# Down products of a gated feed-forward layer: seven products in two pairs of PSUM banks in place of eight, with the order of four engines and the DMA queue given by a table

## The chip, the cores and the metric

The kernel runs on one core of a Trainium2 chip. The core has a matrix engine (TensorE, PE in the profile, with its weight loads as PEld), a vector engine (VectorE, DVE), an activation engine (ScalarE, ACT), a general engine (GpSimd, POOL) and a queue that issues transfers (SyncE, SP). The time is the device time of one execution in microseconds, the median of several runs. All engines run their own instructions in order and wait for each other by semaphores.

## The reference, cut to what matters

The layer mixes an attention branch and a feed-forward branch by a gate `g` per token. There are 2048 tokens of width D = 576, and the hidden width is F = 4608.

```python
g = _sigmoid((x * gate_w).sum(-1, keepdims=True))
a = _A_ref(x, A_wq, A_wk, A_wv, A_wo, A_beta)     # 32 heads, 4 chunks of 512 tokens, a memory carried along
b = (_gelu(x @ w_gate) * (x @ w_up)) @ w_down
return g * a + (1 - g) * b
```

The change is about the last product of `b`, the down product: a 2048 x 4608 matrix (hidden) by a 4608 x 576 matrix (`w_down`), and about how the factor `1 - g` gets onto it.

## The kernel before, in words

Every float32 operand is carried as a pair of 16-bit words, a high one and a low one, and a product is three matmuls: high by high, high by low, low by high. ACT makes the high word (a copy to 16 bits), POOL or DVE the low word (the source minus the high word).

The first part (up to about 210 us) projects queries, keys and values and forms the recurrent memory. The second part is the feed-forward layer with the attention of the 32 heads laid between its work. It is a loop over 72 steps `v`: the hidden width is cut into 36 slices `f` of 128 columns, the tokens into two pairs `p` of chunks of 512, and step `v` has slice `v // 2` and pair `v % 2`. Two slices, so four steps, are a block (`fb` in the code), and there are 18 blocks. The third part multiplies by `wo` and adds the attention branch.

In a step the products of gate and up with both chunks are already formed with seven products in place of eight (names S1 to S4, A11, A12, A22 over the accumulators V, X, Y in the banks V, G, U). Of these, A12 of every block but the first is itself split again into seven products of width 256 in place of eight (`nested`, line 385, with its sums on DVE at lines 1392 to 1406 and its weight sums on POOL at lines 323 to 342). DVE then multiplies gate and up (`hidden`, line 1250), and `hidden_pair` makes the two 16-bit words of each 128 x 512 piece of the hidden matrix (ACT line 1254, POOL line 1255): eight pieces in a block.

The down product of a block runs during the next block. It is 32 chains (`down`): 16 tiles of 128 tokens by two halves of 288 columns, each of six matmuls (two slices by three word products; line 1228) into one bank (`dn`, two buffers). DVE adds each chain into the result `acc` in SBUF, scaled by `ev`, which holds the power-of-two scales and the factor `1 - g` of each token (line 1236).

Beside this lie, in each block: the weights of the next slices (load, sums of squares on ACT line 94, scaling on POOL lines 303, 309 and 432, sums on POOL lines 406 to 410, words on ACT line 418 and POOL line 426; `w_down` words on ACT line 436 and POOL line 440), and four heads, each with two units of scores, softmax and values (scores line 1137, mask and maximum on DVE line 1140, the bound `mb` on ACT line 1150, the exponentials on ACT line 1153, words on ACT line 1163 and POOL line 1164, a transposing transfer on SP, values line 1183, and normalization on DVE lines 1193 to 1200).

The order of the work on PE, ACT, DVE and POOL is the order in which the code of `step` is written (a manual schedule); the DMA queue is ordered by a scheduler.

## Time and profile before

| | |
|---|---|
| Time, median of 3 runs | 1556.04 us (1555.63 to 1557.02) |
| The profiled execution's own span | 1553.8 us |
| PE busy | 1548.4 us (100%) |
| POOL busy | 1305.8 us (84%) |
| DVE busy | 1229.3 us (79%) |
| ACT busy | 1183.7 us (76%) |
| Granted TensorE clock | 1.000 |

The profile was taken from one execution, whose span from the first to the last instruction is 1553.8 us; the median of the runs is 2.2 us above it. A group row gives the line, the engine, the operation, the tiles it writes and reads, the shape and the count; behind the bar the busy time and the mean time of one instruction. An instruction can begin before the one ahead of it on its engine has ended, so the step from start to start can be shorter than the time of one. The steps of the loop repeat block by block: every fourth step begins 72.43 us after the one four before it.

### The profile page before, as it was taken

The page shows a single profiled execution, that of the slowest core. Times are in us where ns is not written, and L with a number is a line of the kernel's source. Part 1 is how long each engine was busy: PE and PEld are TensorE (multiplying, and loading weights), DVE is VectorE, ACT ScalarE, POOL GpSimd, SP SyncE. Part 2 cuts the span into 40 slices and gives each one's busy share as a digit, 9 for nine tenths or more (in the row PEclk, how much of TensorE's full clock was granted, in tenths as well). Part 3 has the DMA queues.
Part 4 walks back from the last instruction along what each step waited for, and adds up shares of the span by engine and source line. Part 5 has one row for each costly group of instructions (what it writes and reads, how often), then busy time and mean ns, then how long its engine had stood idle before and what let it go on. Part 6 is the DMA issues. An engine that isn't in the chain of part 4 may idle for free.

```text
span 1553.8 us, 33925 instructions
## 1 busy us (share of the span) xinstructions
PE 1548.4 (100%) x12195; PEld 955.7 (62%) x12196; DVE 1229.3 (79%) x3198; ACT 1183.7 (76%) x2037; POOL 1305.8 (84%) x1313
## 2 busy tenths in 40 slices
PE   9999999999999999999999999999999999999999
PEld 5665655666666566666666665666666666666577
DVE  6788976778878887878788887878787878887665
ACT  7567544888888888888888888888888888876421
POOL 3544778899898999989899989898999989899597
PEclk9999999999999999999999999999999999999999
DMA  7533341667768687778777878878687878774654
GB/s 254 195 127 125 132 150 34 122 126 140 133 131 141 130 144 130 144 126 137 132 136 126 140 139 136 135 140 151 127 138 133 144 128 141 130 136 99 120 118 138
DMA packets 472601, 210.14 MB, mean 135 GB/s; under 512 B 427632, under 2 KB 437360, under 8 KB 471920
## 3 DMA queue, kind: packets, MB, share of 16 engines
q1 hardware_dynamic: 472432, 207.97, 67.6%
q8 instruction: 96, 1.57, 0.4%
q14 instruction: 73, 0.60, 0.1%
HBM read 92.03 MB, written 27.26 MB: 77 GB/s over the span
## 4 chain that ended last, share of the span: by engine, by line
PE 94%; POOL 3%; ACT 2%; DVE 1%; issue 1%; POOLq 0%
PE dn L1228 27%; PE U L1268 22%; PE V L1268 12%; PE pv L1183 4%; PE G L385 3%; PE st L447 3%; PE dn L454 2%; PE U L1275 2%; PE dn L385 1%; PE U L447 1%; PE V L1280 1%; PE G L1280 1%; PE st L1137 1%; PE G L447 1%; PE st L1669 1%; PE V L1275 1%
## 5 line engine op out<-in xcount | busy, mean ns | idle before, releaser
L1228 PE MATMUL dn<-paird,hh 128*128 128x288 f16 x3396 | 476.5, 286 | 0.2
L1164 POOL TENSOR_TENSOR pf<-pf,ph 128x512 f16<-128x512 f32 (+1 forms) x256 | 359.2, 1403 | 94.6 <-ACT ph L1163 83.6
L1228 PEld LDWEIGHTS <-hh 128*128 128x128 f16 x3456 | 332.2, 98 | 139.1 <-issue 18.1
L1268 PEld LDWEIGHTS <-pairg 128*128 128x128 f16 x2616 | 244.0, 98 | 254.8 <-issue 18.3
L1236 DVE SCALAR_TENSOR_TENSOR acc<-dn,ev,acc 128x288 f32<-128x288 f32 x534 | 274.4, 515 | 51.4 <-PE dn L1228 42.9
L1153 ACT ACTIVATE pf<-pf,mb,esc 128x512 f32<-128x512 f32 (+3 forms) x512 | 293.0, 642 | 5.2
L1268 PE MATMUL U<-xt,pairg 128*128 128x512 f16 x864 | 209.9, 379 | 0.2 <-DVE gl L1459 0.2
L1268 PE MATMUL U<-x,pairg 128*128 128x512 f16 x840 | 204.1, 379 | 0.0
L426 POOL TENSOR_TENSOR pairg<-raw,pairg 128x640 f16<-128x640 f32 (+2 forms) x144 | 176.2, 1239 | 3.0 <-ACT pairg L418 1.5
L1163 ACT ACTIVATE ph<-pf 128x512 f16<-128x512 f32 (+1 forms) x256 | 172.4, 720 | 0.0
L1255 POOL TENSOR_TENSOR hh<-gl,hh 128x512 f16<-128x512 f32 x144 | 164.4, 1163 | 7.5 <-ACT hh L1254 7.5
L1140 DVE CUSTOM_DVE_ANT_0 pf<-st,mask 128x512 f32<-128x512 f32 (+1 forms) x256 | 157.2, 614 | 0.0
L418 ACT ACTIVATE pairg<-raw 128x640 f16<-128x640 f32 (+2 forms) x144 | 89.3, 647 | 56.6 <-POOL raw L410 36.2
L1258 ACT ACTIVATE gl<-gl,sc 128x512 f32<-128x512 f32 x144 | 97.2, 716 | 40.7 <-DVE gl L1505 30.1
L303 POOL TENSOR_SCALAR raw<-raw,sc 128x640 f32<-128x640 f32 x72 | 118.7, 1663 | 0.0
L1459 DVE COPY gl<-U 128x512 f32<-128x512 f32 x72 | 49.8, 692 | 85.4 <-PE U L1268 74.9
L1150 ACT ACTIVATE mb<-mx,esc 128x4 f32<-128x4 f32 x128 | 37.5, 293 | 103.4 <-DVE mx L1140 103.4
L1140 DVE CUSTOM_DVE_ANT_0 pf<-dn,mask 128x256 f32<-128x256 f32 (+1 forms) x192 | 67.2, 375 | 55.3 <-PE dn L1137 55.3
L1268 PE MATMUL V<-xt,pairg 128*128 128x512 f16 x432 | 105.7, 381 | 0.0
L1268 PE MATMUL V<-x,pairg 128*128 128x512 f16 x432 | 104.8, 378 | 0.0
L1254 ACT ACTIVATE hh<-gl 128x512 f16<-128x512 f32 x144 | 82.6, 616 | 16.0 <-DVE gl L1250 15.8
L1183 PEld LDWEIGHTS <-pt 128*128 128x128 f16 x2560 | 83.4, 96 | 12.3
(354 smaller groups left out, 2971.1 us busy)
## 6 DMA issues: line engine op xcount, KB each, us to landing
raw<-in_wgu_dram SPq DMA_DIRECT2D x36, 640.0 KB
rawd<-in_wd_dram SPq DMA_DIRECT2D x36, 288.0 KB
qk<-stage SPq DMA_DIRECT2D x36, 256.0 KB
qt<-qk SPq DMA_DIRECT2D x128, 72.0 KB
kt<-qk SPq DMA_DIRECT2D x128, 72.0 KB
...
qt<-qk SPq DMA_DIRECT2D x128, 36.0 KB
```

The source lines that it names most:

```text
L303: pool.tensor_scalar(r, r, scl[f // 2][0][:, 0:1], None, OP.mult)
L426: pool.tensor_tensor(spot(f, *p, 1), raw_g[f][:, p[0] : p[1]], spot(f, *p, 0), OP.subtract)
L1140: dve.tensor_tensor_reduce(prob[a][:, COL[qi] : COL[qi] + (qi + 1) * P], out[qi], mask[:, L - (qi + 1) * P :], 1.0, -3e38, OP.add, OP.max, ...
L1153: act.activation(r, r, AF.Exp, bias=b[:, qi : qi + 1], scale=esc[:, 0, c : c + 1])
L1163: act.activation(h[:, cols], p[:, cols], AF.Copy)
L1164: pool.tensor_tensor(p.bitcast(F16)[:, cols], p[:, cols], h[:, cols], OP.subtract)
L1183: pe.matmul(ov, pr[:, 10 * i + COL[qi] // P + kb], v[:, 4 * e + kb, c0 : c0 + VC], start=kb == 0 and i == 0, stop=kb == qi and i == 1)
L1228: pe.matmul(o[:, :NH], hh[:, a, q * P : (q + 1) * P], w[:, b, n * NH : (n + 1) * NH], start=i == 0, stop=i == 5)
L1236: dve.scalar_tensor_tensor(av, o[:, :NH], ev, av, OP.mult, OP.add)
L1255: pool.tensor_tensor(hh[:, 1], t, hh[:, 0], OP.subtract)
L1258: act.activation(t, o, AF.Gelu_apprx_tanh, scale=scl[f // 2][0][:, 2 + c : 3 + c])
L1268: pe.matmul(o, w[:, i, (a + k) * P : (a + k + 1) * P], x[:, b + k], start=start and k == 0 and i == 0 and b == h, stop=k == 1 and i == 1, ...
```

## The change: what it does

**Down product.** The pieces of the hidden matrix of a block are, for each chunk pair, a 2 x 2 arrangement (two chunks by two slices), and so are the two slices of `w_down` (two slices by two column halves). The change multiplies them with seven products in place of eight. The sums on the hidden side are four subtractions or additions of 128 x 512 float32 tiles on DVE for each pair (`sums_h`: S3, S2, S1, S4), both inputs in SBUF; the sums on the weight side are four of 128 x 288 on POOL (`down_weights`: t1 to t4). Each of the seven operands on either side gets its two words: on the hidden side 14 in a block on ACT (line 1290) and POOL (line 1294), on the weight side 7 of 128 x 288 in a block (lines 1349 and 1352).

**Banks.** A product (`multiply`) takes two tiles of 128 tokens at once, six matmuls of width 288 into the two banks of a pair: P1, P6, P7 and P4 into the pair `two`, P5, P3 and P2 into the pair `st2`. In each pair the next product is added on top of the one before it in PSUM, and after every product DVE adds what stands there into one quadrant of `acc` (`evict`, 128 x 2 x 288, line 1328). The two pairs of banks replace the banks `dn` and `st`, and the scores of the heads use them too.

**Gate at the end.** The scale in an eviction is now one number per chunk (`we`), and the factor `1 - g` is multiplied into `acc` at the end by 16 activations on ACT (`weigh`, line 1672).

**What moves between engines.** The second split of A12 is dropped: A12 is six matmuls of width 512 again, and a copy from bank G to bank U on DVE stands where the nested sums were. The scaling of the weights goes from POOL to ACT (lines 331 and 372). The bound `mb` goes from ACT to DVE as a three-operand instruction with a constant tile in SBUF (line 1094). The scratch `z` of the scale computation moves from SBUF into a PSUM bank. Loading a head's queries and keys is 12 transfers in place of 8. Some of the output stage's sums go from POOL to DVE.

**Order.** The work of a block is cut into 341 named units, and a table gives their order, with an offset of blocks for units of the block before or after. The order holds for PE, ACT, DVE, POOL and now the DMA queue up to unit A12.1 of the last block, and behind that the scheduler orders all; the output stage's first 14 steps may start between the last down products.

```diff
+ORDER_OF_BLOCK = """
+S3.0 ldg.1 P1.00+1 EP1.00+1 h1.3+1 mb.6+1 sq1.1 tr.5+1 pH.A11.1+1 A11.0 P2.00+1 EP2.00+1 P6.00+1 EP6.00+1
+wL.T3+1 ldd.0 cY.0 va.4+1 P2.01+1 pL.A22.0+1 pH.A22.1+1 wL.T4+1 e3.6+1 pL.S3.1+1 P7.00+1 pH.S1.0+1 cV.0
...
         if fb:
...
-            ev = wts.tile([P, 16], F32, name="ev", tag="ev", bufs=2)
-            pool.tensor_tensor(ev.rearrange("p (c q) -> p c q", c=4),
-                               gate[:, 1].rearrange("p (c q) -> p c q", c=4),
-                               w.unsqueeze(2).to_broadcast([P, 4, 4]), OP.mult)
-            evs[fb - 1] = ev
+            ev = evs[fb - 1] = wts.tile([P, 4], F32, name="we", tag="we", bufs=4)
+            pool.tensor_scalar(ev, scl[fb - 1][1][:, 0], v[:, 0, 1:2], 2.0**35, OP.mult, OP.mult)
...
+    def scale_g(f, parts=(0, 1)):
         if f < NF:
+            for i in parts:
+                r = raw_g[f][:, i * KW : (i + 1) * KW]
+                act.activation(r, r, AF.Copy, scale=scl[f // 2][0][:, 0:1])
...
     def scale_d(f):
         r = raw_d[f]
-        pool.tensor_scalar(r, r, scl[f // 2 + 1][0][:, 1:2], None, OP.mult)
+        act.activation(r, r, AF.Copy, scale=scl[f // 2 + 1][0][:, 1:2])
...
+        def bound(a):
+
+            b = bounds[a] = ap_.tile([P, 4], F32, name="mb", bufs=2)
+            c = 2 * (a // (2 * H)) + a % 2
+            dve.scalar_tensor_tensor(b, mx.pop(a), esc[:, 1, c : c + 1], ln256, OP.mult, OP.add)
...
-        def down(fb, t, n):
-            c, q = divmod(t, 4)
-            o = spare()
-            i = 0
-            for f in (2 * fb, 2 * fb + 1):
-                w = pair_d[f]
-                hh = hp[f, c]
-                for a, b in ((0, 0), (0, 1), (1, 0)):
-                    pe.matmul(o[:, :NH], hh[:, a, q * P : (q + 1) * P], w[:, b, n * NH : (n + 1) * NH],
-                              start=i == 0, stop=i == 5)
-                    i += 1
-            av = acc[:, t, n * NH : (n + 1) * NH]
-            ev = evs[fb][:, t : t + 1]
...
-                dve.scalar_tensor_tensor(av, o[:, :NH], ev, av, OP.mult, OP.add)
...
+            def copy_y():
+                s["Y"] = bank("U")
+                dve.tensor_copy(s["Y"], s["X"])
...
+            def third():
+                a, d = made[b, p, 0, 0], made[b, p, 0, 1]
+                h["A11"], h["S3"] = a, d
+                dve.tensor_tensor(d, a, d, OP.subtract)
+
+            def second():
+                h["S2"] = h["S3"]
+                dve.tensor_tensor(h["S2"], made[b, p, 1, 1], h["S3"], OP.subtract)
+
+            def one():
+                h["S1"] = h["A11"]
+                dve.tensor_tensor(h["S1"], h["S2"], h["A11"], OP.add)
+
+            def fourth():
+                h["S4"] = made[b, p, 1, 0]
+                dve.tensor_tensor(h["S4"], h["S4"], h["S2"], OP.subtract)
...
+        SEVEN = {"P1": ("A11", "B11", 0, 0), "P6": ("S2", "T2", 0, 1), "P7": ("S3", "T3", 1, 1), "P4": ("A22", "T4", 1, 0),
+                 "P5": ("S1", "T1", 1, 1), "P3": ("S4", "B22", 0, 1), "P2": ("A12", "B21", 0, 0)}
...
+            def multiply(m):
+                o = two if m in ("P1", "P6", "P7", "P4") else st2
+                x, w = as_pair(hp[b, p, SEVEN[m][0]]), wp[b, SEVEN[m][1]]
+                for j in range(2):
+                    for k, (g, h) in enumerate(((0, 0), (0, 1), (1, 0))):
+                        pe.matmul(o[:, j, :NH], x[:, g, (q + j) * P : (q + j + 1) * P], w[:, h],
+                                  start=k == 0 and m in ("P1", "P5", "P2"), stop=k == 2, skip_group_check=True)
+
+            def evict(m):
+                e, to = SEVEN[m][2:]
+                t = 4 * (2 * p + e) + q
+                o = two if m in ("P1", "P6", "P7", "P4") else st2
+                o, av = o[:, :, :NH], acc[:, t : t + 2, to * NH : (to + 1) * NH]
+                ev = evs[b][:, 2 * p + e : 2 * p + e + 1]
+                if (t, to) in begun:
+                    dve.scalar_tensor_tensor(av, o, ev, av, OP.mult, OP.add)
...
+            for n, k in enumerate((("B12", "B12", "B11"), ("B22", "B22", "B12"), ("B11", "B22", "B11"), ("B21", "B21", "B22"))):
+                add(f"t{n + 1}", lambda k=k: minus(*k))
...
+        def weigh(ts):
+            for t in ts:
+                act.activation(acc[:, t], acc[:, t], AF.Copy, scale=gate[:, 1, t : t + 1])
...
+        with tc.manual_schedule(engines=ORDERED | {mybir.EngineType.SP}):
+            for k in todo[first:free]:
+                run(k)
```

**Where instructions stand.** VectorE in the middle of a block, before the change. `acc<-dn` is a down eviction, `pf` and `mx` are the masked scores and their maximum, `gl<-U` and `gl<-V` are sums of the gate and up products.

```order
L1236 SCALAR_TENSOR_TENSOR acc<-dn,ev,acc 128x288
L1140 ISA pf_2624,mx<-dn,mask 128x256
L1140 ISA mx 128x1
L1505 TENSOR_TENSOR gl<-U,gl 128x512
L1514 TENSOR_TENSOR gl<-V,gl 128x512
L1140 ISA pf_2624,mx<-pv,mask 128x128
L1140 ISA mx 128x1
L1236 SCALAR_TENSOR_TENSOR acc<-dn,ev,acc 128x288
L1140 ISA pf_2624,mx<-st,mask 128x512
L1140 ISA mx 128x1
L1236 SCALAR_TENSOR_TENSOR acc<-dn,ev,acc 128x288 x2
```

VectorE behind the scores of a unit, after the change. Line 1094 is the bound `mb`, line 1271 the sum S3 of a chunk pair (both inputs are hidden tiles in SBUF), line 1240 the sums of the gate and up products, line 1328 a down eviction.

```order
L1094 SCALAR_TENSOR_TENSOR mb<-mx,esc,ln_76 128x4
L1271 TENSOR_TENSOR hh_2619<-hh_2623,hh_2619 128x512
L1240 TENSOR_TENSOR hh_2621<-U,hh_2621 128x512
L1240 TENSOR_TENSOR hh_2630<-V,hh_2630 128x512
L1328 SCALAR_TENSOR_TENSOR acc<-two_2650,we,acc 128x2x288
L1141 TENSOR_REDUCE pv<-pv 128x144
L1142 RECIPROCAL ord<-pv 128x8
L1145 SCALAR_TENSOR_TENSOR pv<-pv,gha,ord 128x72 x2
L1148 TENSOR_TENSOR ob<-ob,pv 128x8x18
L1328 SCALAR_TENSOR_TENSOR acc<-two_2650,we,acc 128x2x288
L1271 TENSOR_TENSOR hh_2620<-hh_2629,hh_2620 128x512
L1175 SCALAR_TENSOR_TENSOR hh_2630<-G,sc,hh_2630 128x512
```

The evictions are fewer and twice as wide, and between them stand two kinds of instruction that VectorE did not have: the sums of hidden tiles and the bound.

GpSimd at the beginning of a step, before the change. Line 1255 is the low word of a hidden piece, line 303 the scaling of a slice's weights, line 1164 the low words of the attention weights, lines 426 and 336 the low words of the weights and of the second split's sums, lines 406 and 407 the weight sums.

```order
L1255 TENSOR_TENSOR hh_2618<-gl,hh_2618 128x512
L1255 TENSOR_TENSOR hh_2620<-gl,hh_2620 128x512
L303 TENSOR_SCALAR raw<-raw,sc 128x640
L303 TENSOR_SCALAR raw<-raw,sc 128x256
L1164 TENSOR_TENSOR pf_2625<-pf_2625,ph 128x512
L1164 TENSOR_TENSOR pf_2625<-pf_2625,ph 128x768
L426 TENSOR_TENSOR pairg_11843<-raw,pairg_11843 128x640
L426 TENSOR_TENSOR pairg_11843<-raw,pairg_11843 128x384
L336 TENSOR_TENSOR pairg_11843<-nu_2804,pairg_11843 128x128
L406 TENSOR_TENSOR raw<-raw 128x256
```

GpSimd at the turn from one block to the next, after the change. Line 1294 is the low word of a hidden piece or sum, line 1352 that of a down weight, line 1355 a sum of down weights, lines 1112 and 368 the low words of the attention weights and of the gate and up weights.

```order
L1294 TENSOR_TENSOR hh_2626<-hh_2619,hh_2626 128x512
L1355 TENSOR_TENSOR rawd_2331<-rawd_2332,rawd_2331 128x288
L1112 TENSOR_TENSOR pf_2655<-pf_2655,ph 128x768
L1352 TENSOR_TENSOR wp_2643<-rawd_2331,wp_2643 128x288
L1352 TENSOR_TENSOR wp_2637<-rawd_2331,wp_2637 128x288
L1294 TENSOR_TENSOR hh_2632<-hh_2621,hh_2632 128x512
L1352 TENSOR_TENSOR wp_2641<-rawd_2332,wp_2641 128x288
L1294 TENSOR_TENSOR hh_2635<-hh_2620,hh_2635 128x512
L368 TENSOR_TENSOR pairg_9891<-raw,pairg_9891 128x640
```

The scaling instructions are gone from the queue, and the low words and sums of the down product have taken their places.

883 lines of the change are left out of this document (419 added, 464 removed).

## The prediction

> **What bounds the kernel now.** I read the page's busy shares first, then the busy time of two neighbouring blocks, then the chain of work that ended last inside one.
>
> ```profile
> span 1553.8 us, 33925 instructions
> PE 1548.4 (100%) x12195; PEld 955.7 (62%) x12196; DVE 1229.3 (79%) x3198; ACT 1183.7 (76%) x2037; POOL 1305.8 (84%) x1313
> ```
>
> ```profile
> core 0: us, PE busy (x) PEld busy (x) DVE busy (x) ACT busy (x) POOL busy (x), PEclk, DMA share, GB/s
> 410.00:482.43 72.43, 72.43 (x604) 44.24 (x603) 59.20 (x163) 61.90 (x106) 65.90 (x65) 1.00 0.71 135
> 482.43:554.86 72.43, 72.43 (x604) 44.21 (x603) 59.19 (x163) 61.90 (x106) 65.86 (x65) 1.00 0.76 134
> ```
>
> PE is busy all through a block at full clock; POOL has 6.5 us of slack in it, ACT 10.5, DVE 13.2. A busy PE need not be at its peak, so its pace is read from the chain, which is all PE there:
>
> ```profile
> 427.96 1.29 PE U L1268 x6
> 429.47 2.24 PE dn L1228 x18
> 469.41 0.66 PE G L385 x6
> ```
>
> A matmul of width 512 takes 0.215 us from start to start, one of 288 0.124, one of 256 0.11: the rows follow each other without holes. PE sets the time, and only less PE work can shorten the loop, as long as no other engine then needs more than PE.
>
> **PE, what goes and comes.** Of the block's 32 x 6 = 192 matmuls of width 288, 168 stay (4 x 7 products of six): 24 x 0.124 = 2.98 us less. The second split of A12 goes: 42 matmuls of width 256 (4.6 us) become 24 of 512 (5.2 us), 0.5 us more. Block: 72.43 - 2.98 + 0.54 = **70.0 us**. Everything else on PE stays.
>
> **DVE.** Its rows, by shape, and four rows of the timeline for the step from start to start:
>
> ```profile
> L1236 DVE SCALAR_TENSOR_TENSOR acc<-dn,ev,acc 128x288 f32<-128x288 f32 x534 | 274.4, 515 | 51.4 <-PE dn L1228 42.9
> L1250 DVE SCALAR_TENSOR_TENSOR gl<-U,sc,gl 128x512 f32<-128x512 f32 x72 | 53.7, 746 | 3.1 <-PE U L1275 3.1
> L1505 DVE TENSOR_TENSOR gl<-U,gl 128x512 f32<-128x512 f32 x72 | 49.5, 687 | 7.6 <-PE U L1280 5.3 <-PE U L1275 2.4
> L1405 DVE TENSOR_TENSOR nu<-U,nu 128x512 f32<-128x512 f32 x34 | 23.5, 692 | 6.7 <-PE U L1268 6.6
> L1396 DVE TENSOR_TENSOR G<-U,nu 128x256 f32<-128x256 f32 x34 | 14.7, 432 | 1.2
> L1197 DVE SCALAR_TENSOR_TENSOR pv<-pv,gha,ord 128x72 f32<-128x72 f32 x128 | 38.5, 301 | 4.6
> ```
>
> ```profile
> 299.34 0.69 DVE L1505 TENSOR_TENSOR gl<-U,gl 128x512 f32<-128x512 f32 x1
> 299.95 0.68 DVE L1514 TENSOR_TENSOR gl<-V,gl 128x512 f32<-128x512 f32 x1
> 300.75 0.51 DVE L1234 TENSOR_SCALAR acc<-dn,ev 128x288 f32<-128x288 f32 x1
> 301.18 0.68 DVE L1140 CUSTOM_DVE_ANT_0 pf<-st,mask 128x512 f32<-128x512 f32 x1
> ```
>
> An instruction costs 0.08 us less than it lasts when another follows: 0.61 at 512, 0.43 at 288. Removed in a block: 32 evictions, 13.8 us; the sums of the second split, two steps of five at 256 (10 x 0.43) and two steps of two at 512 (4 x 0.70), 7.1 us. Added: 28 evictions of 576 elements. From 288 to 512 an instruction grows by 0.231 us, so 576 lasts 0.81 and costs 0.73: 20.5 us. Four copies from G to U and eight sums of hidden tiles at 0.61: 7.3 us. Eight bounds of four elements, by the row of 72 elements less 0.07: 0.23 each, 1.9 us. Sum: 59.2 - 20.9 + 29.7 = **68.0 us** before any wait of a new kind. That is 2 us under PE, where it was 13.
>
> **The new kind of wait.** The eight sums and eight bounds are DVE instructions with two tensors from SBUF; nearly all others on DVE read at most one from there. The kernel before has few of these, and they show what happens beside POOL:
>
> ```profile
> 413.09 0.73 POOL L406 TENSOR_TENSOR raw<-raw 128x256 f32<-128x256 f32 x1
> 413.55 0.90 DVE L1212 SCALAR_TENSOR_TENSOR oh<-ob,wsc,oh 128x576 f16<-128x576 f32 x1
> 413.91 1.13 POOL L407 TENSOR_TENSOR raw<-raw 128x256 f32<-128x256 f32 x1
> ```
>
> ```profile
> L1212 DVE SCALAR_TENSOR_TENSOR oh<-ob,wsc,oh x16: 809/898/1052, 413.5 to 1447.0; 128x576 f16<-128x576 f32 x16
> L486 DVE SCALAR_TENSOR_TENSOR xt<-acc,xsc,xt x6: 1275/1556/1940, 111.2 to 192.1; 128x1024 f16<-128x1024 f32 x6
> L267 DVE TENSOR_SCALAR pb<-z x19: 170/1080/1116, 160.9 to 1435.0; 128x4 int32<-128x4 int32 x19
> ```
>
> Line 1212 begins while POOL is inside line 406 and lasts 0.90 us in place of 0.81; POOL's next one, begun beside it, lasts 1.13 in place of 0.73. Line 486 lasts 1.28 to 1.94. The two hold each other up: the one that comes second waits for the first to end, and 0.18 of the wait is hidden in the beginning of the DVE instruction (POOL ends 0.27 behind its start, it loses 0.09). Even four elements can lose 0.91 us (line 267, of another kind, with one tensor). The price per instruction lies between 0 and 0.91; nearest are 0.09 (line 1212, the only one inside the loop) and 0.28 (line 486, middle of its six). I take the mean, 0.19, for all sixteen: 3.0 us, so **DVE needs 71.0 us**, more than PE. It becomes the bound. Since PE and DVE then release each other's banks with hardly any slack, I add 0.6 us, the middle between nothing (before, PE never waited) and 1.2 (an estimate: one eviction and a half): **71.6 us a block**.
>
> The Trainium skill's page "SBUF — State Buffer", section "Who interferes with whom", states this as a rule: a VectorE instruction with two SBUF inputs and a GpSimd instruction that reads SBUF exclude each other for a whole instruction, whoever begins first. The rows of lines 486 and 1212 agree. By that rule the bounds of four elements wait just as long as the sums; if instead only wide ones waited, the sum for DVE would be 69.5 us, below PE.
>
> **POOL and ACT, which could take over.**
>
> ```profile
> L1255 POOL TENSOR_TENSOR hh<-gl,hh 128x512 f16<-128x512 f32 x144 | 164.4, 1163 | 7.5 <-ACT hh L1254 7.5
> L303 POOL TENSOR_SCALAR raw<-raw,sc 128x640 f32<-128x640 f32 x55 | 103.4, 1890 | 0.0
> L432 POOL TENSOR_SCALAR rawd<-rawd,sc 128x576 f32<-128x576 f32 x36 | 61.6, 1723 | 0.0
> L426 POOL TENSOR_TENSOR pairg<-raw,pairg 128x384 f16<-128x384 f32 x36 | 33.5, 931 | 0.0
> L440 POOL TENSOR_TENSOR paird<-rawd,paird 128x576 f16<-128x576 f32 x36 | 46.0, 1279 | 0.0
> L323 POOL TENSOR_TENSOR junk<-raw 128x128 f32<-128x128 f32 x17 | 8.5, 502 | 0.0
> ```
>
> ```profile
> L1254 ACT ACTIVATE hh<-gl 128x512 f16<-128x512 f32 x144 | 82.6, 616 | 16.0 <-DVE gl L1250 15.8
> L418 ACT ACTIVATE pairg<-raw 128x640 f16<-128x640 f32 x72 | 52.5, 729 | 38.6 <-POOL raw L410 36.2 <-POOL raw L303 2.4
> L436 ACT ACTIVATE paird<-rawd 128x576 f16<-128x576 f32 x36 | 23.9, 667 | 0.0
> L1150 ACT ACTIVATE mb<-mx,esc 128x4 f32<-128x4 f32 x128 | 37.5, 293 | 103.4 <-DVE mx L1140 103.4
> ```
>
> POOL loses the scaling (by width about 7.8 us, and 2 x 1.72), the second split's six small instructions (some 3.2), two low words of `w_down` (2.6) and the gate's `ev` (0.2): 17.2. It gains six low words more (7.0), seven of width 288 (0.76 each by the rows at 384 and 576: 5.3) and four sums of that width (about 0.8: 3.2): 15.5. So 64.2, and with eight sums of DVE that hold it up by 0.4 each, 67.4 us. ACT gains six high words (3.7), seven of width 288 (0.43: 3.0), four scalings of 640 (2.9) and two of 576 (1.3); it loses the bounds (2.3), two words of `w_down` (1.3) and two of the split (0.8): 61.9 + 6.5 = 68.4 us. Both stay under 71.6 but above 94% of it, so a late DVE also makes them late: POOL's low word waits for DVE's sum, and PE's product for the low word.
>
> **Costed at nothing.** In the block of the scales, `z` in PSUM takes away one wait like line 267's, but the next instruction of four elements stands in SBUF and meets it. Twelve transfers a head in place of eight move the same bytes; DMA is busy 0.71 to 0.76, and what hides them is that a head is loaded a block ahead. Behind a transposing transfer in SP's queue wait the loads of heads and weights; if that cover is gone, PE waits at the values.
>
> **Ends.** The loop with heads is 16 blocks. The last block's steps have no heads, and PE bounds them: 2.4 us less. The last down products stand alone behind the gates: 28 x 0.745 for 32 x 0.745, 3.0 less; the 16 activations for the gate and the chain sum, high word, low word, product at the end cost between nothing and 6 us, since the output stage's first steps stand between: I take 3. Together 2.4 less.
>
> **Sum.** 1553.8 + 16 x (71.6 - 72.43) - 2.4 = 1538.1 us of span; the median lies 2.2 above the profiled span, so 1540.3: forecast **1541 us**, 1.0% faster. For this case alone, 1525 to 1552.
>
> **Rivals.**
> *Slower: DVE waits anywhere inside POOL's instructions.* POOL has 65 instructions in 65.9 us, 1.0 us each, and is busy nine tenths of the time. Starts that fall anywhere in them meet half of one, 0.5 us, less the hidden 0.18: 0.32 each, 5.1 a block. DVE then needs 73.1, and with 0.6 for handing over 73.7: 1553.8 + 16 x 1.3 - 2.4 + 2.2 = 1574 us. It decides from 0.25 us per instruction on, where 68.6 + 16 x 0.25 meets the old block. For it: line 486's upper half. Against it: the loop repeats exactly, so each instruction meets POOL at one phase, and line 1212's costs 0.09. At 0.375 each it is 1588. Chance 0.39. This is what the page's rule gives if nothing lines the two engines up.
> *Full gain: PE stays the bound.* If the waits fall into the 2 us that DVE has, a block is 70.0 and 0.3 for handing over: 16 x 2.1 less, 1520 us. Against it: DVE had 13 us of slack when PE never waited. Chance 0.13.
> *No change*, the waits near 0.25: 1553 to 1559. Chance 0.09.
> *The banks as a loop of their own*: a product (0.75), the way to DVE (0.2), an eviction (0.81) and the way back follow one another on the pair `two`, 16 x 1.85, and eight scores at some 1.2: 39 us of 70. This is not a bound, and I give it no chance of its own.
> That the change doesn't do what it says is excluded by the count: the new order has 3024 down matmuls for 3456.
>
> **How the numbers follow.** Forecast 0.39, full gain 0.13, no change 0.09, slower 0.39. A measurement of this kernel tells about 0.2% from no change. Faster 0.52, same 0.09, slower 0.39. The range goes from below the full gain, 1516, to the slower case at 0.375 us per wait, 1588.
>
> **What would show it.** In the block: PE busy falling below the block's length, with waits of PE for DVE at the down products; DVE busy above 95%; the sums (line 1271 and the three behind) and the bounds (line 1094) lasting longer than 0.69 and 0.23 us, by 0.19 in the mean; POOL near 67 and ACT near 68 us. If sums and bounds show their bare times and PE still waits, the reason is another: the order of the table or a late transfer. If PE is busy throughout, the full gain came.

## The result and the profile after

The changed kernel takes 1605.7 us (median of 4 runs, 1603.1 to 1611.4), the kernel before 1556.5 beside it: ratio 1.032 (95% interval 1.031 to 1.034), so 3.2% slower where 1.0% faster was forecast; also outside the range. The profiled execution has a span of 1600.9 us, 47.1 more than before.

```profile
span 1600.9 us, 32993 instructions
PE 1547.9 (97%) x11458; PEld 868.6 (54%) x11458; DVE 1451.2 (91%) x3249; ACT 1304.4 (81%) x2197; POOL 1291.7 (81%) x1308
```

PE is as long busy as before, with 737 matmuls fewer, and now stands still for 53 us. A yardstick that both kernels have is the copy of accumulator V from PSUM on DVE (line 1339 before, line 1217 after; "V copy" below), once in each step. Read by it the 47.1 us are:

| Stretch | before | after | difference |
|---|---|---|---|
| start, to the copy in the first step of the second block | 251.5 us | 261.9 us | +10.4 |
| 16 blocks | 1159.9 us | 1165.2 us | +5.3 |
| the last three steps | 52.1 us | 56.4 us | +4.3 |
| from the last copy to the end | 90.3 us | 117.4 us | +27.1 |

The yardstick itself has moved. In the first step of every block the new order puts the copy 7.5 to 7.7 us behind the start of the product that it copies (before: 1.6 to 1.8), so some 6 of the 10.4 us are the copy's new place and no lost time; they are missing in the third row. The starts of that product don't have this fault (those of the second block and of the last step; before, then after):

```profile
249.96 1.46 PE L1268 MATMUL V<-xt,pairg 128*128 128x512 f16 x6
1461.52 1.47 PE L1268 MATMUL V<-xt,pairg 128*128 128x512 f16 x6
```

```profile
254.44 1.46 PE L1185 MATMUL V<-xt,pairg 128*128 128x512 f16 x6
1480.55 1.47 PE L1185 MATMUL V<-xt,pairg 128*128 128x512 f16 x6
```

By them the start lost 4.5 us, the 16 blocks 5.3 as in the table, the last three steps 9.2 and the time behind them 28.1.

**A block.** The busy time of two neighbouring blocks, columns as in the prediction:

```profile
406.97:479.73 72.76, 72.01 (x563) 39.05 (x561) 70.52 (x164) 67.94 (x113) 66.28 (x66) 1.00 0.67 134
479.73:552.50 72.77, 71.39 (x559) 38.71 (x557) 70.23 (x163) 67.46 (x112) 65.74 (x66) 1.00 0.60 132
```

Most blocks last 72.75 us, some 73.3. Laid out by starts of matmuls, the first of these blocks has 68.5 us of matmuls at their own pace (before: 70.8), 2.8 us of holes where the height of the operands changes (before: 1.6) and 1.5 us of waits (before: none). So 2.4 us came out of the block, as forecast, and 2.7 came in.

The changes of height are seen in the timeline of PE (start, duration, line, shape). Before:

```profile
425.40 0.38 PE L1275 MATMUL U<-x,pairg 128*128 128x512 f16 x1
425.71 0.39 PE L1280 MATMUL V<-x,pairg 64*128 64x512 f16 x1
425.72 0.39 PE L1280 MATMUL U<-x,pairg 64*128 64x512 f16 x1
425.94 0.38 PE L1137 MATMUL st<-kt,qt 54*128 54x512 f16 x2
```

After:

```profile
522.08 0.38 PE L1192 MATMUL U<-x,pairg 128*128 128x512 f16 x1
522.39 0.39 PE L1197 MATMUL V<-x,pairg 64*128 64x512 f16 x1
522.39 0.39 PE L1197 MATMUL U<-x,pairg 64*128 64x512 f16 x1
522.71 0.91 PE L1318 MATMUL two<-wp,hh 128*128 128x288 f16 x6
```

The height is the number of rows of a matmul's operands. From a matmul of 128 rows to one of 64 the step is 0.31 us in place of 0.215, in both kernels. Before, the scores with their 54 rows always stood directly behind, at 0.22. After, a down product with 128 rows follows 6 times of 8, at 0.32, and most scores stand alone and pay for a change of their own. The table cut these neighbours apart; that is 1.2 us a block, summed from the longer steps (no run puts the neighbours back). (The Trainium skill's page "TensorEngine Tiling (Array Packing)", section "Key Properties", says that changing the tiling mode drains the engine. The rows agree where 128 rows stand beside 64 or 54, at 0.10 us a change; from 64 to 54 rows nothing is lost, 0.22 for 0.215.)

**The end.** PE's waits from 1440 us on (before: none at all):

```profile
PE two L1318 <- DVE acc L1328: 12.7, 9, 6.7
PE G L1615 <- DVE hh L1175: 5.6, 1, 5.6
PE V L1615 <- DVE acc L1624: 3.9, 1, 3.9
PE pv L1615 <- POOL x L1608: 2.0, 1, 2.0
PE V L1185 <- DVE hh L1217: 1.2, 2, 1.0
PE two L1318 <- POOL wp L1352: 1.2, 1, 1.2
```

They sum to 28.7 us with the small ones. The longest, with the slow matmuls behind it, is most of the 9.2 us of the last three steps; nearly all the others fall behind the last V copy. The longest is followed back through three queues, PE, DVE and SP:

```profile
1449.43 1.64 PE L1318 MATMUL two<-wp,hh 128*128 128x288 f16 x12
1458.24 3.04 PE L1318 MATMUL two<-wp,hh 128*128 128x288 f16 x12 [6.66 <-DVE acc L1328]
```

```profile
1446.46 1.54 DVE L1283 TENSOR_TENSOR hh<-hh,hh 128x512 f32<-128x512 f32 x1
1456.69 0.17 DVE L1551 TENSOR_SCALAR wst<-wst 128x5 f32<-128x5 f32 x1 [8.69 <-ACT junk L120]
1457.38 1.53 DVE L1328 SCALAR_TENSOR_TENSOR acc<-two,we,acc 128x576 f32<-128x576 f32 x2
```

```profile
1440.17 12.79 SPq L1546 DMA_DIRECT2D raw<-in_wo_dram x3
```

Line 1551 scales the sums of squares of `wo`. It needs ACT's squares, these need the load of `wo`, and the load's third part waits 11.2 us until POOL's words of the weights have freed its buffer. Behind the 128 x 5 instruction stand the evictions that PE waits for. In the kernel before, the engines keep the order of the code at the end too; here the scheduler put the instruction there.

The wait costs twice. Twelve down matmuls last 1.64 us ahead of it and 3.04 behind it, and the windows show the granted TensorE clock as a share of full speed (the third number from the end):

```profile
1450.00:1455.00 5.00, 1.58 (x29) 1.30 (x28) 0.00 (x0) 2.59 (x6) 5.00 (x6) 1.00 0.26 56
1455.00:1460.00 5.00, 1.76 (x8) 1.14 (x8) 2.94 (x6) 1.23 (x3) 0.94 (x1) 0.52 0.67 137
1510.00:1515.00 5.00, 2.11 (x9) 1.24 (x9) 2.74 (x4) 0.63 (x1) 5.00 (x7) 0.50 0.33 106
1535.00:1540.00 5.00, 5.00 (x22) 3.16 (x21) 3.79 (x6) 1.71 (x3) 4.39 (x5) 0.50 0.31 59
```

The clock is 0.50 to 0.52 behind each of the three longest waits (6.66, 5.62 and 3.88 us), and behind the fourth, 3.48 us at 1493, the 3.4 us from 1492.8 are at 0.50 too. In the kernel before it is 1.00 to the end. The Trainium skill's page "TensorE: Matmul & The Clock Gate", section "What's actually happening", gives the rule: half the clock behind an idle window of about 3.4 us, for about as long. These four waits agree. A run below shows that a shorter wait, 2.75 us, can be enough.

**The new kind of wait.** One line of code each, durations min/median/max in ns:

```profile
L1271 DVE TENSOR_TENSOR hh<-hh,hh x36: 677/934/1664, 243.1 to 1469.7; 128x512 f32<-128x512 f32 x36
L1283 DVE TENSOR_TENSOR hh<-hh,hh x36: 675/1324/1540, 256.3 to 1524.6; 128x512 f32<-128x512 f32 x36
L1094 DVE SCALAR_TENSOR_TENSOR mb<-mx,esc,ln x128: 211/492/1503, 281.1 to 1433.3; 128x4 f32<-128x4 f32 x128
L1328 DVE SCALAR_TENSOR_TENSOR acc<-two,we,acc x488: 798/808/821, 259.9 to 1560.2; 128x576 f32<-128x576 f32 x163
L303 DVE TENSOR_SCALAR pb<-pb x19: 155/157/162, 160.7 to 1466.1; 128x4 int32<-128x4 int32 x19
```

```profile
L1094 DVE SCALAR_TENSOR_TENSOR mb<-mx,esc,ln 128x4 f32<-128x4 f32 x128 | 60.4, 472 | 1.7
L1283 DVE TENSOR_TENSOR hh<-hh,hh 128x512 f32<-128x512 f32 x36 | 46.2, 1283 | 1.1 <-POOL hh L1294 1.1
L1271 DVE TENSOR_TENSOR hh<-hh,hh 128x512 f32<-128x512 f32 x36 | 37.3, 1035 | 0.0
L1279 DVE TENSOR_TENSOR hh<-hh,hh 128x512 f32<-128x512 f32 x36 | 35.5, 987 | 0.0
L1275 DVE TENSOR_TENSOR hh<-hh,hh 128x512 f32<-128x512 f32 x36 | 28.6, 795 | 0.0
```

A sum (lines 1271 to 1283) lasts 1.03 us in the mean, 0.35 over its shortest; a bound (line 1094) 0.47, 0.26 over its shortest. With eight of each that is 4.9 us a block. The eviction lasts 0.81, always.

### The profile page after: what moved, and what is told of

It reads as the page before. It is cut to its first block, busy times and chain, and to the rows that moved or that the text cites. A ratio compares the mean times of both kernels' runs of the same rounds, so it can differ in the third digit from the quotient of the medians.

```text
span 1600.9 us, 32993 instructions
## 1 busy us (share of the span) xinstructions
PE 1547.9 (97%) x11458; PEld 868.6 (54%) x11458; DVE 1451.2 (91%) x3249; ACT 1304.4 (81%) x2197; POOL 1291.7 (81%) x1308
## 4 chain that ended last, share of the span: by engine, by line
ACT 32%; PE 30%; DVE 13%; issue 8%; POOL 7%; DMA 5%; SPq 4%; POOLq 0%; ACTq 0%
ACT pf L1101 9%; PE two L1318 7%; PE U L1185 5%; ACT ph L1108 4%; DVE acc L1328 3%; ACT L1178 3%; ACT hh L1178 3%; SPq L1040 3%; PE G L1185 3%; PE V L1185 2%; DVE pf L1083 2%; ACT hh L1290 2%; DMA kt<-qk 2%; POOL pf L1112 2%; ACT L1101 2%
## 5 line engine op out<-in xcount | busy, mean ns | idle before, releaser
L1318 PE MATMUL two<-wp,hh 128*128 128x288 f16 x3024 | 438.6, 288 | 28.3 <-DVE acc L1328 23.6
L1328 DVE SCALAR_TENSOR_TENSOR acc<-two,we,acc 128x576 f32<-128x576 f32 x488 | 385.5, 810 | 9.7 <-PE two L1318 8.5
L1294 POOL TENSOR_TENSOR hh<-hh,hh 128x512 f16<-128x512 f32 x252 | 313.5, 1253 | 8.7 <-ACT hh L1290 8.6
L1101 ACT ACTIVATE pf<-pf,mb,esc 128x384 f32<-128x384 f32 (+3 forms) x512 | 298.6, 642 | 17.2 <-POOL hh L1294 8.4
L1083 DVE CUSTOM_DVE_ANT_0 pf<-two,mask 128x384 f32<-128x384 f32 (+2 forms) x448 | 210.5, 511 | 3.6 <-PE two L1080 3.6
L1185 PE MATMUL G<-x,pairg 128*128 128x512 f16 x864 | 209.9, 379 | 0.5 <-DVE hh L1175 0.5
L368 POOL TENSOR_TENSOR pairg<-raw,pairg 128x640 f16<-128x640 f32 (+2 forms) x144 | 178.3, 1240 | 14.3 <-ACT pairg L363 14.3
L1290 ACT ACTIVATE hh<-hh 128x512 f16<-128x512 f32 x252 | 151.2, 615 | 17.1 <-DVE hh L1279 9.2
L1178 ACT ACTIVATE hh<-hh,sc 128x512 f32<-128x512 f32 x144 | 99.8, 715 | 37.8 <-DVE hh L1456 19.4
L1101 ACT ACT_TABLE_LOAD x64 | 82.1, 1283 | 52.6 <-issue 52.0
L1352 POOL TENSOR_TENSOR wp<-rawd,wp 128x288 f16<-128x288 f32 x126 | 99.7, 803 | 11.2 <-ACT wp L1349 11.1
L1185 PE MATMUL U<-x,pairg 128*128 128x512 f16 x432 | 105.1, 379 | 1.3 <-DVE hh L1467 0.8
L1178 ACT ACT_TABLE_LOAD x65 | 83.4, 1283 | 1.2
```

The costliest lines, as they stand in the source:

```text
L368: pool.tensor_tensor(spot(f, *p, 1), raw_g[f][:, p[0] : p[1]], spot(f, *p, 0), OP.subtract)
L1083: dve.tensor_tensor_reduce(prob[a][:, COL[qi] : COL[qi] + (qi + 1) * P], out[qi], mask[:, L - (qi + 1) * P :], 1.0, -3e38, OP.add, OP.max, ...
L1101: act.activation(r, r, AF.Exp, bias=bounds[a][:, qi : qi + 1], scale=esc[:, 0, c : c + 1])
L1178: act.activation(t, o, AF.Gelu_apprx_tanh, scale=scl[f // 2][0][:, 2 + c : 3 + c])
L1185: pe.matmul(o, w[:, i, (a + k) * P : (a + k + 1) * P], x[:, b + k], start=start and k == 0 and i == 0 and b == h, stop=k == 1 and i == 1, ...
L1290: act.activation(as_pair(hp[b, p, k])[:, 0], of(k), AF.Copy)
```

## The experiments

All are edits of the changed kernel. "Rest" is the time from the last V copy to the end in the profile; the changed kernel has 117.4 us there and a usual block of 72.75. The loop varies from execution to execution: in the profiles of the runs that change the end alone its 16 blocks take 1164.7 to 1169.4 us, and 1176.5 in one that has a block of 80.3. Differences of a few us in the whole time therefore say little; blocks and rests say more.

### The loop: is VectorE the bound?

**The eight sums left out.**

```diff
 def third():
-    dve.tensor_tensor(d, a, d, OP.subtract)
+    pass
 # and the same in second, one, fourth
```

> The changed kernel without the eight sums of hidden tiles on VectorE (S3, S2, S1 and S4 of both chunk pairs are left out; the words are made of the unsummed tiles). VectorE is rid of eight instructions of 1.03 us in the mean, from start to start about 0.97, so 7.8 us a block, among them the chain from sum to sum. Theory 'VectorE sets the block': the block falls to what TensorE needs, 70.0 to 70.6 us, over 16 blocks 34 to 44 us: 1562 to 1572 us. Rival 'the order and the ways set it': less than half of that, above 1586 us.

Measured: 1606.8 us (ratio 1.031 to 1.034). A block:

```profile
479.70:552.40 72.70, 72.08 (x563) 39.02 (x562) 64.19 (x156) 67.76 (x112) 63.36 (x66) 1.00 0.59 130
```

DVE has 6 us less to do and the block is as long as ever. PE's waits sum to 1.5 us as before, in other places. DVE's total is not the bound. (The rest is 124.3 us here, 6.9 longer; what lengthens it isn't known.)

**The four scalings of the gate and up weights on ACT left out.**

```diff
 def scale_g(f, parts=(0, 1)):
-    act.activation(r, r, AF.Copy, scale=scl[f // 2][0][:, 0:1])
+    pass
```

> The changed kernel without the four scalings of the gate and up weights on ScalarE (line 331 is left out; the words are made of the unscaled weights). ScalarE is rid of four instructions of 0.73 us, 2.9 us a block; three of them lie where ScalarE waits for the next unit's exponentials soon after. Theory 'way from engine to engine': the block falls by less than 0.7 us, since the scalings do not lie on the chain: above 1592 us. Rival 'ScalarE is full' (66.5 us of instructions and 10.3 us of table loads and waits in 72.75): the block falls by what is taken away until TensorE bounds it, to 71.2 us or less, 1578 to 1582 us.

Measured: 1605.7 us (1.030 to 1.033). ACT is busy 64.9 us in a block of 73.30, and blocks last 73.3 to 73.8: no shorter, with less work. Blocks of 73.3 are no sign of the edit: the run below with eight products in the last block alone has the changed kernel's loop and shows them in 10 of its 16 blocks. ACT's total isn't the bound either.

**The bound back on ACT**, undoing that part alone.

```diff
-dve.scalar_tensor_tensor(b, mx.pop(a), esc[:, 1, c : c + 1], ln256, OP.mult, OP.add)
+act.activation(b, mx.pop(a), AF.Copy, bias=LN256, scale=esc[:, 1, c : c + 1])
```

> The changed kernel, with the bound of the exponentials on ScalarE again as in the kernel before, in place of VectorE. VectorE is rid of eight instructions of 0.46 us in the mean (3.7 us a block), ScalarE gains about eight times 0.27 (66.5 to 68.7 us a block). Theory 'VectorE with its waits for GpSimd sets the block': the block falls from 72.75 to between 70.4 and 71.3 us (TensorE needs 70.0), over 16 blocks 23 to 38 us: 1568 to 1583 us. Rival 'the order of the table and the way from engine to engine set it': the block stays within 0.4 us of 72.75, or grows because the exponentials now wait for ScalarE: above 1598 us.

Measured: 1654.3 us (1.058 to 1.068), most blocks 75.4, some 77 and 82. In this order of the work, made for DVE, the move to DVE helps.

**The bound with one tensor from SBUF.**

```diff
-dve.scalar_tensor_tensor(b, mx.pop(a), esc[:, 1, c : c + 1], ln256, OP.mult, OP.add)
+dve.tensor_scalar(b, mx.pop(a), esc[:, 1, c : c + 1], LN256, OP.mult, OP.add)
```

> The changed kernel with the bound of the exponentials on VectorE as an instruction with one tensor from SBUF and a constant as second operand, in place of two tensors (line 1094, four elements). What it tells is what such a small instruction waits for beside GpSimd. If only instructions with two tensors from SBUF and GpSimd exclude each other, line 1094 lasts 0.15 to 0.25 us throughout in place of 0.21 to 1.50 (mean 0.46), and VectorE is rid of 2 us a block; if one tensor waits as well (line 267 of the kernel before did, up to 1.12 us), it lasts as before. The time: by the theory 'way from engine to engine' up to 0.7 us a block less, since the bound lies on the chain at two places, 1594 to 1606 us; if it waits as before, 1602 to 1608 us.

Measured: 1608.9 us (1.029 to 1.038), and the bound waits just as long:

```profile
L1094 DVE TENSOR_SCALAR mb<-mx,esc x128: 218/504/1504, 281.0 to 1441.4; 128x4 f32<-128x4 f32 x128
```

So the second tensor is not what makes it wait.

**The maxima in PSUM**, in four columns of the banks `two` that the scores leave free, and the bound with one tensor.

```diff
-mx[a] = ap_.tile([P, 4], F32, name="mx", bufs=2)
+mx[a] = two[:, a % 2, 500:504]
```

> The changed kernel with the four maxima of a unit kept in PSUM (columns 500 to 503 of the pair two, which nothing else uses) in place of SBUF, and the bound made of them by one operand and a constant, so that it reads no tensor from SBUF. The waits of the bound for GpSimd should vanish: line 1094 lasts 0.47 us in the mean (0.21 to 1.50) and should last 0.15 to 0.25. Theory 'the bound's waits lie on the way from scores to exponentials and lengthen the block': 0.3 to 0.6 us each at two or three units, block 71.5 to 72.4 in place of 72.75, 1586 to 1600 us. Rival 'several ways of nearly the same length, so no single one counts': within 0.25 us a block, 1601 to 1609 us.

Measured: 1720.6 us (1.100 to 1.111).

```profile
L1094 DVE TENSOR_SCALAR mb<-two,esc x128: 203/214/224, 281.9 to 1544.0; 128x4 f32<-128x4 f32 x128
```

```profile
PE two L1318 <- DVE two L1083: 44.2, 48, 4.9
PE two L1080 <- DVE mb L1094: 21.3, 30, 1.1
```

With its input in PSUM the bound never waits. But PE now waits for the maxima and for the bound, since they stand in the banks of the down products: blocks of 79.4 us. What the bound's waits for POOL cost the block can't be read from this run.

**Less work on all three engines**: sums, scalings and ten weight sums on POOL left out.

```diff
-pool.tensor_tensor(g2, g0, g2, OP.add)   # and four more per slice
-act.activation(r, r, AF.Copy, scale=...)  # six per block
-dve.tensor_tensor(d, a, d, OP.subtract)   # and seven more per block
```

> The changed kernel with work taken from three engines at once and none from TensorE: the eight sums of hidden tiles on VectorE (7.8 us a block), all six scalings on ScalarE (4.2 us) and the ten sums of the gate and up weights on GpSimd (7 us) are left out. Taken alone the first left the block at 72.72 us and the second gave 73.3. Theory 'several ways from engine to engine of nearly the same length, each long enough': with all of them shorter the block falls to what TensorE needs, between 70.6 us (its matmuls with the holes that it has without any wait) and 71.6: 16 times 1.2 to 2.1, so 1572 to 1588 us. Rival 'something that none of the three has, TensorE's own holes or the transfers, sets 72.7': the block stays above 72.3 us, above 1597 us.

Measured: 1671.9 us (1.073 to 1.077), most blocks 77.9: the opposite. The timelines of DVE and POOL show one reason (line 1085 is the bound here, lines 1103 and 1285 the low words of attention and hidden pieces):

```profile
646.16 3.57 DVE L1085 SCALAR_TENSOR_TENSOR mb<-mx,esc,ln 128x4 f32<-128x4 f32 x1
649.65 0.68 DVE L1231 TENSOR_TENSOR hh<-V,hh 128x512 f32<-128x512 f32 x1
```

```profile
645.83 1.18 POOL L1103 TENSOR_TENSOR pf<-pf,ph 128x512 f16<-128x512 f32 x1
646.94 1.18 POOL L1285 TENSOR_TENSOR hh<-hh,hh 128x512 f16<-128x512 f32 x1
648.05 1.66 POOL L1103 TENSOR_TENSOR pf<-pf,ph 128x768 f16<-128x768 f32 x1
```

The bound begins inside POOL's first instruction and ends, 3.57 us later, with its third (648.05 + 1.66 = 649.71). One instruction of four elements waited for three, because POOL had no gap between them; up to 4.27 us in this run. With its other work gone POOL's low words stand back to back. PE's timeline shows what follows:

```profile
651.12 1.12 PE L1309 MATMUL two<-wp,hh 128*128 128x288 f16 x6 [2.75 <-DVE acc L1319]
652.03 2.76 PE L1176 MATMUL G<-x,pairg 128*128 128x512 f16 x6
```

The eviction behind the bound is late, PE waits 2.75 us for it, and the next six matmuls last 2.76 us in place of 1.46: the clock is 0.51 from 651.6 to 655.0. Such a wait of 2.7 us comes 15 times, and the clock halves behind ten of them. Most blocks with the halved clock last 77.9 us, most without it 76.3, so 1.6 of the 5 us are the clock.

**The maxima in PSUM on top of this.**

> The run e12 (sums of hidden tiles, all scalings and the sums of the gate and up weights left out: 77.5 us a block, 66 us slower than with them) with the bound read from PSUM. In e12 the bound of one unit lasts 3.6 us in the mean and up to 4.3, and ends with GpSimd's third instruction behind its start. Theory 'VectorE's wait for GpSimd lasts as long as GpSimd has instructions without a hole, and that is what made the lighter kernel slower': the bound lasts 0.15 to 0.25 us, the block falls to between 70.6 and 72.3 us, and the kernel to 1572 to 1592 us. Rival 'the phases of the queues, whatever their cause': the block stays above 75 us, above 1630 us.

Measured: 1684.5 us (1.081 to 1.084), blocks of 77.9. The bound lasts 0.2 us again, and PE's waits for the maxima and the bound in its banks (39.4 and 22.0 us over the run) took the place of its wait, so the share of either isn't separated.

**Eight entries of the table moved**, so that bounds meet POOL elsewhere.

```diff
-P1.00+1 EP1.00+1 h1.3+1 mb.6+1 sq1.1 tr.5+1 ... EP2.00+1
+P1.00+1 EP1.00+1 sq1.1 tr.5+1 ... EP2.00+1 h1.3+1 mb.6+1
-cY.3 mb.4
+mb.4 cY.3
```

Moved likewise are `a0.3` (ahead of `P3.11+1`) and `wH.B11 wH.T4 pH.S2.0 wH.T2` (behind `g1.3`).

> The changed kernel with eight words of the table moved and not an instruction added or removed: unit a0.3 next to a1.3, ahead of two evictions; wH.B11, wH.T4, pH.S2.0 and wH.T2 behind the GELU units g0.3 and g1.3; h1.3 and mb.6 behind the eviction EP2.00; cY.3 behind the bound mb.4. Without the sums (run e5) the block kept its 72.72 us though VectorE was busy 64 us of it, and the chain of waits there goes from TensorE to VectorE (masks, h0.2), to ScalarE (13.5 us of exponentials, words and then GELU) and by h0.3, the masks and the evictions EP1.00 and EP2.00 back to TensorE. Theory 'way from engine to engine': the moves take 1.5 us each out of that chain at two places, and the block falls to between 71.2 and 72.2 us (TensorE: 70.0 us of matmuls at their usual pace and about 1.1 us of small holes between unlike matmuls), 9 to 25 us over 16 blocks: 1580 to 1597 us. Rivals 'an engine is full' (VectorE or ScalarE by their sums): within 0.25 us of 72.75 a block, 1602 to 1610 us.

Measured: 1601.3 us (1.027 to 1.030), the best of all. A bound lasts 0.31 us in the mean in place of 0.47, 1.3 us less a block; the block is 72.68, 0.07 less, and the rest 114.1. The bounds' waits, as long as they are here, do not set the block.

### The end: the order or the work?

**Line 1551 one stage later** (in the code, from stage 1 of `finish` to stage 2).

```diff
+                dve.tensor_scalar(wst[:, 5:10], wst[:, 0:5], 4.0, None, OP.mult)   # as the first line of the next stage
```

> The changed kernel, with one VectorE instruction of the output stage (five numbers times four, line 1551, which waits for the squares of wo) issued one stage later, so that no eviction stands behind it. Theory 'blocked queue': VectorE's 8.69 us of idle time ahead of this instruction, TensorE's 6.66 us behind it and the slow matmuls after that (3.04 us for twelve in place of 1.64) vanish, and the kernel gets 7 to 9 us faster: about 1597 us. Rival 'too little room at the end': the engines are short of time in the last 150 us anyway (GpSimd is busy throughout from 1490 to 1535 us), the stall only moves to a later place: less than 3 us faster, above 1602 us. The steps of the loop stay at 72.75 us a block in both.

Measured: 1605.6 us (1.029 to 1.034). The scheduler put the instruction back ahead of the evictions, and VectorE waits 8.8 us for it; PE still waits 6.7 us.

**The preparation of the output behind the last gate products**, in the scheduler's order.

```diff
-("S3.1", False, (finish, 0)), ("S2.1", True, (turn, 2)), ("A12.1", True, (finish, 1)),
+("A12.2", False, (finish, 0)), ("S1.2", True, (turn, 2)), ... ("LR.3", True, (finish, 1)),
```

> The changed kernel, with the whole preparation of the output stage set behind the last gate products and spread over the last down products (the load of wo a step and a half later, squares, scales, sums and words behind unit LR.3 of the last block), and with line 1551 later as in the run beside it. Theory 'blocked queue': the stalls of TensorE at 1458, 1493, 1513 and 1535 us (6.66, 3.48, 5.62 and 3.88 us) come from output-stage instructions that wait in the queues of VectorE and ScalarE for transfers and for GpSimd; without them 15 to 25 us of the 28 us that the end lost come back: 1580 to 1590 us. Rival 'too little room at the end': GpSimd then starts the output stage's words later, and what is gained ahead of 1500 us is lost behind it: above 1597 us. The loop stays at 72.75 us a block.

Measured: 1606.3 us (1.030 to 1.034), rest 119.2. Here too the scheduler put the instruction ahead of evictions (VectorE waits 8.3 us for it), so neither run takes away what it was made to take away.

**The same with PE, DVE, ACT and POOL in the order in which the code is written.**

```diff
-with ExitStack():
+with tc.manual_schedule(engines=ORDERED):
```

> The changed kernel with the late preparation of the output stage as in the run before (load of wo, squares, scales, sums and words behind the last gate products, spread over the last down products), and now with the instructions of PE, DVE, ACT and POOL behind unit A12.1 of the last block kept in the order of the program, as the kernel before has it, in place of an order that the scheduler chooses. In the two runs of the tail before, the scheduler had put line 1552 (the squares times four) back ahead of the evictions, where VectorE waited 8.8 and 8.3 us for it, so they did not take the suspected cause away. Theory 'blocked queue': the 6.7 us stall goes, with the slow matmuls behind it, and no engine waits for a transfer with evictions behind it: the part behind the last copy from bank V falls from 117 us by 15 us or more, the kernel to 1575 to 1590 us. Rival 'too little room at the end' (sums, words, evictions and the weighing with 1 - g need the time in any order): less than 5 us, above 1600 us.

Measured: 1636.0 us (1.049 to 1.057). The first wait is gone and the last V copy comes 7 us earlier, but the rest is 157.0: ACT's scaling by `1 - g` stands in its queue 40 us for evictions, with words behind it that PE needs.

**The last block by eight products**, which needs no sums on DVE and POOL there.

```diff
+if b == NB - 1:
+    for m in EIGHT:
+        add(f"{m}.{p}{n}", lambda m=m: multiply8(m))
+        add(f"E{m}.{p}{n}", lambda m=m: evict8(m))
+    return
```

> The changed kernel, with the down product of the last block alone made of eight products again (16 groups of 12 matmuls into the same two pairs of banks, one eviction each, no sums; words of four hidden tiles a pair and of four halves of the weights). In the last block nothing covers the way from sum to word to product any more. Behind the gates TensorE loses 24 matmuls of 0.124 us as gain (3.0 us more work), VectorE is rid of 12 evictions of 0.73 us and 8 sums of about 0.9 (16 us), GpSimd of 6 low words of 1.16, 3 of 0.73 and 4 sums of 0.76 us (12 us), out of about 100 us that each has in the last 160. Theory 'the end is too long a way: sums, words, products and evictions of the last block, one after the other': the kernel gets 8 to 18 us faster, 1588 to 1598 us. Rival 'blocked queue' (output-stage instructions waiting for transfers): the stalls stay where they are, less than 4 us, above 1601 us. Theory 'nothing but the first stall': no change.

Measured: 1603.2 us (1.028 to 1.032), rest 114.6. The interval overlaps that of the changed kernel; the rest is 2.8 us shorter.

**Line 1551 on ACT**, where it can't stand ahead of evictions.

```diff
-dve.tensor_scalar(wst[:, 5:10], wst[:, 0:5], 4.0, None, OP.mult)
+act.activation(wst[:, 5:10], wst[:, 0:5], AF.Copy, scale=4.0)
```

> The changed kernel with the five squares times four of the output stage (line 1551) on ScalarE behind the squares themselves in place of VectorE, so that VectorE doesn't wait for ScalarE, and ScalarE not for anyone new. This takes away what makes VectorE wait 8.7 us at 1448 to 1457 us, which the two earlier runs of the tail had failed to do. Theory 'blocked queue': TensorE's stall of 6.66 us and the slow matmuls behind it (1.4 us) go, 6 to 9 us: 1597 to 1600 us. Rival 'too little room at the end': the later stalls grow by as much, less than 2.5 us, above 1603 us.

Measured: 1604.3 us (1.029 to 1.032), rest 116.3. PE's longest wait at a down product falls to 3.2 us, and almost nothing is gained: in its place PE waits 5.1 us for a transposing transfer that stands behind the load of `wo` in SP's queue.

**Both.**

> Both edits of the two runs before together. If the first stall and the length of the last block's down product are two separate losses, their gains add up: 14 to 27 us, 1579 to 1592 us. If the one only moves what the other takes away, the gain is that of the larger alone.

Measured: 1603.4 us (1.029 to 1.034), rest 113.5. In place of the first wait PE again waits 5.2 us for that transfer. POOL has hardly a gap from 1490 to 1530 us (two of 0.7), with output sums and words of later tiles ahead of the hidden words.

**All five queues in a written order**, `wo` loaded later, line 1551 on ACT, no early output products, with eight products in the last block:

```diff
-out_steps = [(u, p) for u in range(2) for p in (7, 1, 4, 2, 6, 5, 3)]
+out_steps = []
-with ExitStack():
+with tc.manual_schedule(engines=ORDERED | {mybir.EngineType.SP}):
```

> The changed kernel with its end alone changed: behind unit A12.1 of the last block all five queues keep the order of the program (as in the kernel before) in place of one that the scheduler chooses; wo is loaded when its last buffer is free; the output stage's sums and words for the pairs of tiles 2 to 4 stand behind the last down products, as before, and no output product is started ahead of them; the last block's down product is made of eight products (run e9), and line 1551 is on ScalarE (run e10). Those two edits alone gave 2.5 and 1.4 us, and both together 2.3: the profile showed GpSimd busy throughout from 1490 to 1531 us with the output stage's sums and words for later tiles ahead of the words that the last down products needed. Theory 'wrong order at the end': the part behind the last copy from bank V, 117 us, comes back to between 95 and 104 us (before: 90.3 and the 16 weighings), the kernel to 1583 to 1594 us. Rival 'too little room at the end': above 110 us, above 1598 us.

and with seven:

> As the run beside it (order of the program at the end, later output stage, line 1551 on ScalarE), but with the seven products of the change in the last block too. It tells the order from the form of the last down product. If the order alone is the cause, the time is within 4 us of the run beside it. If the way from sum to word to product to eviction is one too, it is slower by 8 to 25 us: 28 products of 0.75 us with an eviction between two in the same pair of banks, 1.85 us each on the pair two, need 30 us in place of 24, and the sums and six more words come ahead of them.

Measured: 1667.0 us (1.069 to 1.073) and 1683.8 us (1.080 to 1.083), rests of 192.0 and 205.7. In both, part of the operand of the last gate product is overwritten by the transposes that stand ahead of it; the work is the same in amount. My order was bad: with eight products PE waits 14.5 us for a transfer at the last gate products, and 11 to 15 us four times in the output stage for evictions; VectorE's queue waits there by way of POOL, which waits 50.6 us for transposing transfers in SP's queue. The two are comparable with each other, and there seven products in the last block cost 16.8 us more than eight: sum, word, product and eviction follow each other with nothing to cover them.

**As in the kernel before**: four queues written, SP's left to the scheduler, transposes and `finish` at their old places, eight products in the last block, line 1551 on ACT, no early output products and the weighing later; then the same with the moved table.

```diff
-("S3.1", False, (finish, 0)), ("S2.1", True, (turn, 2)), ("A12.1", True, (finish, 1)),
+("S1.1", False, (finish, 0)), ("LR.1", True, (turn, 2)), ("S2.2", True, (turn, 2)),
 ...
-with ExitStack():
+with tc.manual_schedule(engines=ORDERED):
```

> The queues of TensorE, VectorE, ScalarE and GpSimd in program order in the last block and the end, SyncE's left to the scheduler as in the kernel before; eight products in the last block; the output's preparation where the kernel before has it, with squares, finishing sums and weighing put behind the steps of gates; the loop as in the change. Theory 'the order at the end is wrong' (the start and the loop cost 19 us, the end 28): the time from the last V copy to the end falls from 117 us to 95 to 104, total 1583 to 1593. Rival 'ScalarE and GpSimd have too little room at the end, in whatever order': the rest stays above 110, total above 1598.

> The same, and in the loop the eight entries of the table moved as in the run with moved words, which was 4.4 us faster than the change. If the two gains add, this is 4 to 5 us below the run beside it: 1579 to 1589 by the theory of the wrong order, above 1594 by the rival.

Measured: 1609.8 us (1.033 to 1.037) and 1607.1 us (1.031 to 1.036); the intervals overlap, so it isn't known whether the loop's gain adds. Waits of PE in the first from 1440 us on:

```profile
PE V L1648 <- DVE acc L1657: 15.0, 1, 15.0
PE two L1355 <- POOL wp L1385: 8.8, 1, 8.8
PE two L1327 <- DVE acc L1337: 5.0, 1, 5.0
PE two L1355 <- DVE acc L1363: 4.4, 5, 0.9
```

The last V copy comes 9 us earlier than in the changed kernel, and the rest is 134.1 us, 17 longer: POOL's words of `w_down` are late by 8.8, and the first output products wait 15.0 for an eviction of the output stage. This meets the bound set for the rival, too little room on ACT and POOL. It doesn't prove it for every order, since each of the three orders written here had a wait of its own that another might not have. Whether an order exists that gives back the 27 us stays open. No run takes the 16 activations for `1 - g` out of the end, so their share is open too.

## Why the prediction was wrong, point by point

The forecast missed the profiled span by 62.8 us (1538.1 against 1600.9): 18.6 in the 16 blocks and 44.2 in the ends.

**The step that failed most: the ends, "Together 2.4 less".** Measured: 41.8 more (10.4 + 4.3 + 27.1). The step costed the tail chain at 0 to 6 us, on the ground that output steps stand between. It counted instructions and didn't ask in which order the scheduler lays them, nor what a wait of several microseconds does to the clock: PE waits 28.7 us from 1440 us on, where it never waited, and runs at half the clock behind the four longest of these waits. The price of the chain alone, seven against eight products in the last block, depends on the order around it: 2.8 us of the rest in the scheduler's order, 16.8 us in the written one. Whether the order or too little room on ACT and POOL makes these waits is not settled. At the start I put down nothing; PE there waits 5.5 us (before 1.6), which is most of the 4.5 us that the start lost.

**PE, 70.0 us a block.** The matmuls were right: 2.37 us less measured, 2.44 worked out. Wrong was "everything else on PE stays": the order of the table cost 1.2 us more in changes of height, so PE's own floor is 71.3, and only 1.5 of the 72.75 us are waits. PE's order was there to be read, and I looked at DVE's and POOL's only.

**DVE becomes the bound at 71.0.** Its busy time is 70.2 to 70.5, close, but by luck, since two errors cancel: the bare work is some 65.6 (worked out 68.0), and the waits 4.9 (worked out 3.0; 0.35 and 0.26 us each for 0.19). That is near the slower rival's 0.32. Yet neither that rival nor the forecast had the mechanism: without the sums DVE falls to 64.2 and the block stays. The largest part of 72.7 is PE's own 71.3. The 1.5 us of waits on top stay, or grow, in the runs with 6 us less on DVE, 3 less on ACT, or 1.3 less of the bounds' waits; I take them for a loop through several engines that wait for each other in order, but no run shows which engines close it.

**The Trainium skill's rule on SBUF** (page "SBUF — State Buffer", section "Who interferes with whom", cited there) holds as far as these runs show: four elements wait as the wide ones do. In the changed kernel the mean wait, about 0.30 us, is the slower rival's half instruction (0.32). Line 1085 shows that this is no upper limit: there POOL's gaps count, not its instructions.

**The loop's length, 71.6 us.** Measured 72.75, between "no change" (72.4) and "slower" (73.7). With the forecast's ends the loop alone would have given a kernel 0.2% slower (+5.3 - 2.4).

**ACT 68.4 and POOL 67.4 us.** Measured 67.5 to 67.9 and 65.7 to 66.3: right, POOL a little high.

**Eviction of 576 elements, 0.81 us.** Measured 0.808. That behind `z` in PSUM "the next instruction of four elements stands in SBUF and meets" the wait was nearly all wrong. Line 302, which reads SBUF again behind the two that read `z`, lasts 169/213/500 ns, so it can wait 0.33 us, far less than line 267's 0.91; line 303 lasts 0.157 us always.

**The banks as a loop of their own**, no chance given: right in the loop. At the end, where PE has nothing else, it shows: the run as in the kernel before has five waits of up to 0.9 us between its last products, 4.4 us in all.

**What would show it.** I named DVE's share above 95% and PE waits at the down products as signs of a DVE bound. Both came (70.5 of 72.76 is 97%), and the theory was still wrong: a busy share that contains waits for POOL looks like work. Only leaving work out told them apart.
